# Finishing attention heads without transposing them: inverse sums spread by DMA, scaling on Pool, outputs kept by head columns

## The chip, the core and the metric

The kernel runs on one core of a Trainium2 chip. The core has engines with a queue of instructions each, taken in order: PE (matrix products; PEld in a profile is its loading of weights), DVE (vector work), ACT (scalar functions and copies), POOL (elementwise work) and SP, which here only issues DMAs. Engines wait for each other by semaphores. The metric is the time on the device in microseconds, the median of the runs.

## The reference

Everything is float32. With S = 2048 tokens, D = 576, 32 heads of 18 columns and F = 4608:

```python
xn = _layernorm(x, axis=-1)
qkv = (xn @ wqkv).reshape(B, S, 3, H, Dh).transpose(2, 0, 3, 1, 4)
scores = jnp.einsum("bhqd,bhkd->bhqk", q, k) * (Dh ** -0.5)
p = _softmax(scores, axis=-1)
o = jnp.einsum("bhqk,bhkd->bhqd", p, v)
s = o.transpose(0, 2, 1, 3).reshape(B, S, D) @ wo
b = ((xn @ w_gate) * (xn @ w_up)) @ w_down
return x + s * _silu(b)
```

## The kernel before

Products with long sums split each float32 operand into a high half (rounded to PE's faster format) and a low half (the rest), and sum three products of halves. There are three stages.

The first normalizes x, computes queries, keys and values, and keeps them in DRAM (tensors `sqk`, `sv`). The second, from about 195 us to 2523 us, does the attention of 32 heads and the gated part together. Its order is planned ahead in Python: a loop follows two PE streams and the engines with fixed costs, and emits one operation after the other; `soon`, `moves`, `jobs` and `due` are its lists of work that comes due at some planned time. The third stage is the output product.

For one head, the second stage does: 64 score products whose row maxima DVE takes (`a_item`, L671 and L673, into PSUM banks "a", of which there are two); 64 transposed score products with the maximum folded in, whose exponentials ACT takes (`b_item`, L723 and L725); and in two or so visits (`pv_group`, L734) the products with the values. In a visit PE does up to eight key tiles in a row, each of PE's four groups of 32 columns taking a chunk of 512 queries, and both streams stop for it, so no other product runs beside. The result of a visit is 128x512: partition 32c + d0 + j holds column j of the head for the 512 queries of chunk c, and partition 32c + d0 + 18 holds their sums of exponentials, since `sv` has a column of ones behind each head's 18. Here d0 is 0 for even heads and 13 for odd ones. The first visit of a head is copied to `oc` by ACT (L738), later ones are added by DVE (L740). Between all this stand the products of the gated part (L779 up and gate, L840 down), with their weights loaded on SP (`wgu`, `wd`); in the first six heads or so these weights are also split into halves and stored.

When a head is complete, `finish` (L744 to L766) is put into `jobs`, and the next visit begins with it: DVE transposes `oc` in blocks of 32 (L748), so that tokens stand on partitions, takes the inverse of the sums (L751) and multiplies (L761, put off until Pool is free) into `ot`, which holds two heads. For every second head four DMAs (L756) write `ot` to `so`, a DRAM tensor of [S, D].

The third stage (from L1372 on) goes through 16 tiles of 128 tokens. `fetch_o` (L1381) loads a tile of `so`; ACT repeats the last 64 columns (`join`, L1409); PE transposes five blocks of 128 columns (`columns`, L1417 and L1419); ACT copies the result as the high half (L1421, L1423) and DVE subtracts it to get the low half (L1422, L1424), both into `oT`. Then PE does 28 matmuls with `wo` (L1440) into two of four banks, DVE multiplies with the silu of the gated part, `gin` (L1450), Pool adds x, `xi` (L1455), and Pool's queue stores the result. The silus of the last four token tiles are worked off in small pieces (`chore`, L924 to L934) during the first nine or so tiles.

Memory is handed out by pools that are stacks: the third stage's tiles lie where the second stage's were, and a load into them waits until the old tile there has been read.

Of the kernel before, what the change touches and what calls it, by code (L numbers as in the profile page):

```python
# [41 lines left out]
def kernel(  # L42
# [35 lines left out]
    so = dram.tile([S, D], FT, name="so")  # L78
# [573 lines left out]
    nc.gpsimd.memset(neg.bitcast(FT), 0.0)  # L652
    with ExitStack() as mid:
# [75 lines left out]
        def pv_group(h, ts, k):  # L729
# [6 lines left out]
            if ts[0] == 0:  # L736
                oc[h] = mp.tile([128, 512], FT, name="oc", bufs=1)
                nc.scalar.activation(oc[h], p, AF.Copy)  # L738
            else:
                nc.vector.tensor_tensor(oc[h], oc[h], p, op=OP.add)  # L740

        def finish(h, now):
# [5 lines left out]
            nc.vector.transpose(od.rearrange("p j d -> p (j d)"), o)  # L748
            rc = mp.tile([128, NT, 1], FT, name="rc", bufs=2)
            d0 = 13 * (h % 2)  # L750
            nc.vector.reciprocal(rc, od[:, :, d0 + DH:d0 + DH + 1])  # L751

            def store():
                o = ot.pop(g).rearrange("p j h d -> p j (h d)")
                for c in range(4):
                    nc.sync.dma_start(  # L756
                        so[512 * c:512 * c + 512, g * 2 * DH:(g + 1) * 2 * DH].rearrange("(j q) c -> q j c", q=32),
                        o[32 * c:32 * c + 32])

            def scale(end):  # L760
                nc.vector.tensor_tensor(ot[g][:, :, hh, :], od[:, :, d0:d0 + DH],  # L761
                                        rc.to_broadcast([128, NT, DH]), op=OP.mult)
# [418 lines left out]
        def visit(now):  # L1181

            ends = [j for j in jobs if j[1] is finish]
            for j in ends:
                jobs.remove(j)
                finish(j[2], engine("DVE", max(now, j[0]), 0.93))
# [9 lines left out]
            if many:  # L1196
# [6 lines left out]
                if ts[-1] == NT - 1:  # L1203
                    jobs.append((end + 0.2, finish, h))
# [81 lines left out]
        def order():  # L1286
# [5 lines left out]
            while going(0) or going(1) or na < TOTAL or nb < TOTAL or due or jobs or soon or pool_later:  # L1292
# [11 lines left out]
                if (need and len(due) >= need and due[need - 1][2] <= now  # L1304
                        or any(j[1] is finish for j in jobs) and nb == TOTAL and not due):
                    wait = now if wait is None else wait
                    both = going(0) and going(1)
                    if abs(clk[0] - clk[1]) < 0.04 and next_free("g") - 0.1 <= now + 0.03 or now > wait + 2.0 or not both:
                        visit(now if both else max([now] + [j[0] for j in jobs] + [d[2] for d in due]))
# [65 lines left out]
    with ExitStack() as end:  # L1375
        ep = end.enter_context(tc.tile_pool(name="end", bufs=1, reuse_waits="tile"))
        oin, gin, xi = {}, {}, {}

        def fetch_o(t):
            oin[t] = ep.tile([128, 640], FT, name="oin", bufs=5)  # L1380
            nc.sync.dma_start(oin[t][:, 0:D], so[t * 128:(t + 1) * 128, :])  # L1381
# [17 lines left out]
        for t in order[:2]:  # L1399
            fetch_o(t)  # L1400
        wo_rest()
        for t in order[2:4]:
            fetch_o(t)
        for t in order[:4]:
# [3 lines left out]
        def join(t):  # L1408
            nc.scalar.activation(oin[t][:, D:640], oin[t][:, 512:D], AF.Copy)  # L1409
# [78 lines left out]
```

## Time and profile before

| | |
|---|---|
| median of 3 runs | 2597.2 us (2596.98 to 2598.14) |
| profiled execution, first to last instruction | 2595.7 us |
| DVE: L748, L751, L761 | x32, mean 702, 254 and 508 ns |
| PE: L1417 and L1419 | x64 and x16 |
| SP: L756 | x64 |

A row of the timeline gives start and duration in us, engine and line, the operation, what it writes and reads, shapes, and in brackets the idle time of its engine before it and what ended it. A row of windows gives, for a stretch of time, its length, then for PE, PEld, DVE, ACT and POOL the busy time and in brackets the number of instructions, then the granted clock of PE, the busy share of the 16 DMA engines, and GB/s. SPq is SP's queue: the time that issuing a DMA takes there.

### The profile page before, as it was taken

The page shows a single profiled execution, that of the slowest core. Times are in us where ns is not written, and L with a number is a line of the kernel's source. Part 1 is how long each engine was busy: PE and PEld are TensorE (multiplying, and loading weights), DVE is VectorE, ACT ScalarE, POOL GpSimd, SP SyncE. Part 2 cuts the span into 40 slices and gives each one's busy share as a digit, 9 for nine tenths or more (in the row PEclk, how much of TensorE's full clock was granted, in tenths as well). Part 3 has the DMA queues.
Part 4 walks back from the last instruction along what each step waited for, and adds up shares of the span by engine and source line. Part 5 has one row for each costly group of instructions (what it writes and reads, how often), then busy time and mean ns, then how long its engine had stood idle before and what let it go on. Part 6 is the DMA issues. An engine that isn't in the chain of part 4 may idle for free.

```text
span 2595.7 us, 59551 instructions
## 1 busy us (share of the span) xinstructions
PE 2588.4 (100%) x24520; PEld 2126.7 (82%) x24520; DVE 1786.6 (69%) x2969; ACT 1546.3 (60%) x3107; POOL 671.4 (26%) x694
## 2 busy tenths in 40 slices
PE   9999999999999999999999999999999999999999
PEld 8899877888887778877777888777787878877889
DVE  7209777766777777777777777777777777777236
ACT  4223677766776656665665766656666666666622
POOL 3114444434431222211111222111221222112015
PEclk9999999999999999999999999999999999999999
DMA  7899767677653435444554444343544453433366
GB/s 242 252 300 257 203 182 197 183 191 215 175 191 108 151 134 173 150 142 158 156 174 131 147 139 142 131 139 131 165 166 116 140 146 130 147 130 119 133 208 211
DMA packets 207696, 435.12 MB, mean 168 GB/s; under 512 B 83168, under 2 KB 132992, under 8 KB 177216
## 3 DMA queue, kind: packets, MB, share of 16 engines
q1 hardware_dynamic: 205264, 423.35, 53.5%
q0 software_dynamic: 2160, 7.96, 0.8%
q8 instruction: 193, 3.16, 0.5%
q14 instruction: 79, 0.65, 0.1%
HBM read 314.64 MB, written 111.35 MB: 164 GB/s over the span
## 4 chain that ended last, share of the span: by engine, by line
PE 97%; DVE 1%; DMA 1%; ACT 0%; issue 0%; ACTq 0%; SPq 0%
PE pg L779 36%; PE pg L734 17%; PE pg L840 16%; PE pa L671 11%; PE pb L723 9%; PE pg L1440 2%; PE pg L520 2%; PE pb L463 2%; PE pa L463 1%; DMA sqk<-hl 1%; DVE st L358 0%; PE pb L1417 0%; DVE xn L369 0%; PE pa L723 0%; PE pb L336 0%; DVE mx L673 0%
## 5 line engine op out<-in xcount | busy, mean ns | idle before, releaser
L673 DVE TENSOR_REDUCE mx<-pa 128x1 f32<-128x512 f32 x2016 | 1350.8, 687 | 356.3 <-PE pb L723 172.5
L725 ACT ACTIVATE pt<-pb 128x512 f32<-128x512 f32 x2001 | 1147.2, 603 | 487.8 <-PE pb L723 385.3
L779 PE MATMUL pg<-xc,wgu 64*128 64x512 f32 x7776 | 1391.9, 392 | 0.1
L779 PEld LDWEIGHTS pg<-xc,wgu 64*128 64x128 f32 x7776 | 1049.9, 186 | 54.1 <-issue 0.8
L840 PE MATMUL pg<-wd,hs 64*128 64x288 f32 x6816 | 822.9, 293 | 0.0
L671 PE MATMUL pa<-whole,turning 54*128 54x512 f32 x1999 | 783.2, 398 | 0.1
L840 PEld LDWEIGHTS pg<-wd,hs 64*128 64x128 f32 x6816 | 773.8, 185 | 9.8 <-issue 0.8
L723 PE MATMUL pb<-whole,turning 56*128 56x512 f32 x1977 | 774.4, 398 | 0.0
L734 PE MATMUL pg<-pt,vt 128*32 128x512 f32 x4096 | 453.3, 594 | 0.1
L820 POOL TENSOR_TENSOR hs<-us,hs 128x512 fp32r<-128x512 f32 x144 | 186.2, 1293 | 980.4 <-ACT hs L804 732.1
L671 PEld LDWEIGHTS pa<-whole,turning 54*128 54x128 f32 x1999 | 363.5, 184 | 78.0 <-issue 53.0
L723 PEld LDWEIGHTS pb<-whole,turning 56*128 56x128 f32 x1977 | 359.6, 184 | 7.0 <-ACT pt L725 0.2
L734 PEld LDWEIGHTS pg<-pt,vt 128*32 128x32 f32 x4096 | 126.2, 110 | 285.5 <-issue 279.2
L867 POOL TENSOR_TENSOR acc<-acc,st 128x288 f32<-128x288 f32 x281 | 227.1, 811 | 488.1 <-ACT st L897 283.8
L740 DVE TENSOR_TENSOR oc<-oc,pg 128x512 f32<-128x512 f32 x35 | 24.1, 687 | 220.8 <-PE pg L734 220.8
L257 POOL TENSOR_TENSOR wgu<-wraw,wgu 128x384 fp32r<-128x384 f32 x108 | 108.2, 1015 | 215.2 <-ACT wgu L256 120.6
L738 ACT ACTIVATE oc<-pg 128x512 f32<-128x512 f32 x32 | 19.2, 598 | 230.2 <-PE pg L734 230.2
L903 DVE TENSOR_TENSOR acc<-acc,pg 128x288 f32<-128x288 f32 x264 | 118.0, 448 | 36.0 <-PE pg L840 32.3
L796 DVE TENSOR_TENSOR us<-pg,us 128x512 f32<-128x512 f32 x144 | 98.3, 683 | 47.7 <-PE pg L779 34.1
L897 ACT ACTIVATE st<-pg 128x288 f32<-128x288 f32 x281 | 115.9, 413 | 24.1 <-PE pg L840 18.0
L789 ACT ACTIVATE us<-pg 128x512 f32<-128x512 f32 x141 | 84.4, 598 | 73.9 <-PE pg L779 60.5
L804 ACT ACTIVATE hs<-us 128x512 fp32r<-128x512 f32 x142 | 89.1, 627 | 11.9 <-DVE us L796 11.8
(150 smaller groups left out, 1293.7 us busy)
## 6 DMA issues: line engine op xcount, KB each, us to landing
wgu<-swg SPq DMA_DIRECT2D x102, 1152.0 KB
wd<-swd SPq DMA_DIRECT2D x50, 1152.0 KB
swg<-wgu SPq DMA_DIRECT2D x36, 1152.0 KB
whole<-sqk SPq DMA_DIRECT2D x192, 144.0 KB
turning<-sqk SPq DMA_DIRECT2D x384, 72.0 KB
swd<-wd SPq DMA_DIRECT2D x18, 1152.0 KB
sqk<-hl SPq DMA_DIRECT2D x32, 512.0 KB
xc<-sx SPq DMA_DIRECT2D x24, 512.0 KB
```

Of the source, the lines that this page charges most:

```text
L257: nc.gpsimd.tensor_tensor(w[:, 9 + b:12 + b, :], raw[:, b:b + 3, :], w[:, b:b + 3, :].bitcast(FT), op=OP.subtract)
L671: nc.tensor.matmul(p, q[rows, t * 128:(t + 1) * 128], k[rows, c * 512:(c + 1) * 512], start=True, stop=True)
L673: nc.vector.tensor_reduce(mx[h][:, t, c:c + 1], p, axis=AX.X, op=OP.max)
L723: nc.tensor.matmul(p, k[rows, t * 128:(t + 1) * 128], q[rows, c * 512:(c + 1) * 512], start=True, stop=True)
L725: nc.scalar.activation(pt[t, c // 2][:, c % 2, :], p, AF.Exp, scale=scale)
L734: nc.tensor.matmul(p[32 * c:32 * c + 32, :], vt[h // 2][:, t, 6 * (h % 2):6 * (h % 2) + 32], pt[t, c // 2][:, c % 2, :], start=t == ts[0], ...
L779: nc.tensor.matmul(ps, gw[n][half[r], a, :], xg[i][half[r], e, :], start=k == 0, stop=k == len(TERMS) - 1)
L820: nc.gpsimd.tensor_tensor(hj[:, 1, :], h32, hj[:, 0, :].bitcast(FT), op=OP.subtract)
L840: op = nc.tensor.matmul(ps[:, 0:HALF], hs[u][half[r], j, a, s * 128:(s + 1) * 128], dw[u][half[r], j, e, i * HALF:(i + 1) * HALF], start=( ...
L867: nc.gpsimd.tensor_tensor(a, a, st, op=OP.add)
L897: nc.scalar.activation(st, ps[:, 0:HALF], AF.Copy)
L903: nc.vector.tensor_tensor(a, a, ps[:, 0:HALF], op=OP.add)
```

## The change

At a head's end nothing is transposed any more. `finish` is called as soon as the last visit's addition is planned, and works with `oc` as it stands, columns on partitions:

1. `collect`: four DMAs on SP bring the four rows of sums (512 numbers each) to a tile of 128x16, `lt`.
2. `invert`: DVE takes the inverses of that tile into `rt`.
3. `keep`: a DMA stores them as a row of a DRAM tensor `srl`.
4. `spread`: four DMAs load that row, each chunk repeated on 18 partitions, into `share`, a 128x512 tile that was filled with ones once.
5. `scaled`: Pool multiplies `oc` by `share`.
6. `store`: four DMAs write the head's 18 rows to `sot`, a DRAM tensor of [D, S].

Each step comes due when the plan takes the step before it as done. `oc` has two buffers instead of one, and the planning loop goes on until every head is stored. In the third stage a tile of `sot` is loaded by three DMAs with the columns already on partitions; `join`, `columns` and the transpositions go, and ACT and DVE split from SBUF (`parts`), two tiles ahead, with three `oT` instead of two. The third stage's pool begins with an unused tile of 6080 numbers, so its other tiles lie elsewhere, and the first loads come in another order.

```diff
-    so = dram.tile([S, D], FT, name="so")
+    sot = dram.tile([D, S], FT, name="sot")
+    srl = dram.tile([H, S], FT, name="srl")
...
+    share = accp.tile([128, 512], FT, name="share")
+    nc.gpsimd.memset(share, 1.0)
...
         def finish(h, now):
-            g, hh = divmod(h, 2)
-            o = oc.pop(h)
-            if hh == 0:
-                ot[g] = accp.tile([128, NT, 2, DH], FT, name="ot", bufs=1)
-            od = mp.tile([128, NT, 32], FT, name="od", bufs=1)
-            nc.vector.transpose(od.rearrange("p j d -> p (j d)"), o)
-            rc = mp.tile([128, NT, 1], FT, name="rc", bufs=2)
-            d0 = 13 * (h % 2)
-            nc.vector.reciprocal(rc, od[:, :, d0 + DH:d0 + DH + 1])
+
+            o, d0 = oc.pop(h), 13 * (h % 2)
+            finishing.add(h)
+            sums_of = mp.tile([128, 16], FT, name="lt", bufs=1)
+            inverse_of = mp.tile([128, 16], FT, name="rt", bufs=1)
+
+            def collect():
+                for c in range(4):
+                    row = 32 * c + d0 + DH
+                    nc.sync.dma_start(sums_of[32 * c:32 * c + 32, :],
+                                      o[row:row + 1, :].rearrange("o (a j) -> o a j", j=16))
+                soon.append((moved(now + 0.1, 0.01) + 1.0, "DVE", 0.15, invert))
+
+            def invert(end):
+                nc.vector.reciprocal(inverse_of, sums_of)
+                move(end + 0.1, lambda: keep(end + 0.1))
+
+            def keep(at):
+                nc.sync.dma_start(srl[h].rearrange("(p j) -> p j", j=16), inverse_of)
+                at = moved(at, 0.01) + 1.0
+                move(at, lambda: spread(at))
+
+            def spread(at):
+                for c in range(4):
+                    row = 32 * c + d0
+                    nc.sync.dma_start(share[row:row + DH, :],
+                                      srl[h:h + 1, 512 * c:512 * c + 512].to_broadcast([DH, 512]))
+                soon.append((moved(at, 0.15) + 1.0, "POOL", 1.30, scaled))
+
+            def scaled(end):
+                nc.gpsimd.tensor_tensor(o, o, share, op=OP.mult)
+                move(end + 0.1, store)
 
             def store():
-                o = ot.pop(g).rearrange("p j h d -> p j (h d)")
                 for c in range(4):
-                    nc.sync.dma_start(
-                        so[512 * c:512 * c + 512, g * 2 * DH:(g + 1) * 2 * DH].rearrange("(j q) c -> q j c", q=32),
-                        o[32 * c:32 * c + 32])
-
-            def scale(end):
-                nc.vector.tensor_tensor(ot[g][:, :, hh, :], od[:, :, d0:d0 + DH],
-                                        rc.to_broadcast([128, NT, DH]), op=OP.mult)
-                if hh == 1:
-                    move(end + 0.1, store)
-
-            soon.append((now, "DVE+", 0.53, scale))
+                    row = 32 * c + d0
+                    nc.sync.dma_start(sot[h * DH:(h + 1) * DH, 512 * c:512 * c + 512], o[row:row + DH, :])
+                finishing.discard(h)
+
+            move(now + 0.1, collect)
...
                 if ts[-1] == NT - 1:
-                    jobs.append((end + 0.2, finish, h))
+                    finish(h, end)
...
+        ep.tile([128, 6080], FT, name="room", bufs=1)
...
         def fetch_o(t):
-            oin[t] = ep.tile([128, 640], FT, name="oin", bufs=5)
-            nc.sync.dma_start(oin[t][:, 0:D], so[t * 128:(t + 1) * 128, :])
+            oin[t] = ep.tile([128, 5, 128], FT, name="oin", bufs=5)
+            tokens = slice(t * 128, (t + 1) * 128)
+            nc.sync.dma_start(oin[t][:, 0:4, :], sot[0:512, tokens].rearrange("(k p) s -> p k s", p=128))
+            for b in (0, 64):
+                nc.sync.dma_start(oin[t][b:b + 64, 4, :], sot[512:576, tokens])
...
-        def columns(t):
+        def parts(t):
             o = oin.pop(t)
-            oc = ep.tile([128, 9, 128], FR, name="oT", bufs=2)
-            oT[t] = oc
-            p = bank("b", 2)
-            for k in range(4):
-                nc.tensor.transpose(p[:, k * 128:(k + 1) * 128], o[:, k * 128:(k + 1) * 128], ident)
...
+            oc = oT[t] = ep.tile([128, 9, 128], FR, name="oT", bufs=3)
+            nc.scalar.activation(oc[:, 0:4, :], o[:, 0:4, :], AF.Copy)
+            nc.scalar.activation(oc[:, 8, :], o[:, 4, :], AF.Copy)
+            nc.vector.tensor_tensor(oc[:, 4:8, :], o[:, 0:4, :], oc[:, 0:4, :].bitcast(FT), op=OP.subtract)
+            nc.vector.tensor_tensor(oc[64:128, 8, :], o[64:128, 4, :], oc[64:128, 8, :].bitcast(FT),
+                                    op=OP.subtract)
```

Lines move by 3 at L671 to L740 (L743 is the old L740, L676 the old L673), by 21 at L779 to L966 and by 7 at L1440 to L1459.

What the plan makes of it on DVE, at the end of one head in the middle (mx: row maxima of the next head; us: the product of up and gate; acc: sums of the down product). Before:

```order
L673 TENSOR_REDUCE mx<-pa 128x1 x6
L740 TENSOR_TENSOR oc<-oc,pg 128x512
L673 TENSOR_REDUCE mx<-pa 128x1 x5
L796 TENSOR_TENSOR us<-pg,us 128x512
L673 TENSOR_REDUCE mx<-pa 128x1 x11
L796 TENSOR_TENSOR us<-pg,us 128x512
L673 TENSOR_REDUCE mx<-pa 128x1 x3
L903 TENSOR_TENSOR acc<-acc,pg 128x288
L673 TENSOR_REDUCE mx<-pa 128x1
L903 TENSOR_TENSOR acc<-acc,pg 128x288
L673 TENSOR_REDUCE mx<-pa 128x1 x12
L748 STREAM_TRANSPOSE od<-oc 128x512
```

And now, for a head in the middle:

```order
L924 TENSOR_TENSOR acc<-acc,pg 128x288
L743 TENSOR_TENSOR oc<-oc,pg 128x512
L676 TENSOR_REDUCE mx<-pa 128x1 x5
L762 RECIPROCAL rt<-lt 128x16
L676 TENSOR_REDUCE mx<-pa 128x1 x12
L817 TENSOR_TENSOR us<-pg,us 128x512
```

Before, more than 30 instructions lie between a head's last addition and its transposition; now five lie between the addition and the reciprocal, which waits for the four collects.

On SP, for the same head now (lt, srl, share and sot are the four steps above; wgu and wd are weights of the gated part, whole and turning queries and keys):

```order
L757 DMA lt<-oc 32x1x16 x4
L287 DMA wd<-swd 128x2304
L766 DMA srl<-rt 128x16
L773 DMA share<-srl 18x512 x4
L323 DMA turning<-sqk 18x1024 x3
L662 DMA vt<-sv 128x16x38
L248 DMA wgu<-swg 128x2304
L323 DMA whole_1180<-sqk 18x2048 x3
L784 DMA sot<-oc 18x512 x4
```

Before, at this place SP had, in one piece and for every second head:

```order
L659 DMA vt<-sv 128x16x38
L322 DMA turning<-sqk 18x1024 x3
L286 DMA wd<-swd 128x2304
L756 DMA so<-ot 32x16x36 x4
L247 DMA wgu<-swg 128x2304
L322 DMA turning<-sqk 18x1024 x3
```

Four DMAs in one place have become thirteen in four places, each of which waits for another engine or for the DMA before it.

On DVE in the third stage, now, from the first two tiles on (gl: a silu of the last four tiles):

```order
L1433 TENSOR_TENSOR oT<-oin,oT 128x512
L1434 TENSOR_TENSOR oT<-oin,oT 64x128
L1457 TENSOR_TENSOR y<-pg,gin 128x288 x2
L948 TENSOR_SCALAR gl<-gl 128x576
L952 RECIPROCAL gl<-gl 128x144
L1433 TENSOR_TENSOR oT<-oin,oT 128x512
L1434 TENSOR_TENSOR oT<-oin,oT 64x128
L1457 TENSOR_TENSOR y<-pg,gin 128x288 x2
L952 RECIPROCAL gl<-gl 128x144 x3
```

The order of the kinds is the old one; the low halves read `oin` in SBUF where they read a PSUM bank (pb, pa).

More of the change, by code (lines that the diff above doesn't have):

```diff
@@ L1181, in visit @@
         def visit(now):
[L1183 to L1186, printed above, removed]
             if not due:
@@ L1303, in order @@
                 need = wanted() if next_free("g") < 1e9 else 0
-                if (need and len(due) >= need and due[need - 1][2] <= now
-                        or any(j[1] is finish for j in jobs) and nb == TOTAL and not due):
+                if need and len(due) >= need and due[need - 1][2] <= now:
                     wait = now if wait is None else wait
@@ L1308, in order @@
                     if abs(clk[0] - clk[1]) < 0.04 and next_free("g") - 0.1 <= now + 0.03 or now > wait + 2.0 or not both:
-                        visit(now if both else max([now] + [j[0] for j in jobs] + [d[2] for d in due]))
+                        visit(now if both else max([now] + [d[2] for d in due]))
                         wait = None
```

30 lines of the change are left out of this document (9 added, 21 removed).

## The prediction

> **What bounds the kernel now.** I read the page first, then the chain of waits, then the timeline around one head's end, then the timeline and the windows of the last 75 us.
>
> ```profile
> span 2595.7 us, 59551 instructions
> PE 2588.4 (100%) x24520; PEld 2126.7 (82%) x24520; DVE 1786.6 (69%) x2969; ACT 1546.3 (60%) x3107; POOL 671.4 (26%) x694
> PE 97%; DVE 1%; DMA 1%; ACT 0%; issue 0%; ACTq 0%; SPq 0%
> ```
>
> PE is busy throughout and is 97% of the chain. DVE is busy for 69% of the span, so time taken off DVE is worth something only where PE stands waiting for DVE. Two places matter: the end of each head, 32 times, and the output product after the last down product (L840). The end of a head in the kernel before, from the timeline (start, duration, engine, line):
>
> ```profile
> 1673.74 0.69 DVE L740 TENSOR_TENSOR oc<-oc,pg 128x512 f32<-128x512 f32 x1 [6.60 <-PE pg L734]
> 1674.35 9.06 DVE L673 TENSOR_REDUCE mx<-pa 128x1 f32<-128x512 f32 x13
> 1675.26 0.39 PE L671 MATMUL pa<-whole,turning 54*128 54x512 f32 x1
> 1675.96 0.39 PE L671 MATMUL pa<-whole,turning 54*128 54x512 f32 x1
> 1676.66 0.40 PE L671 MATMUL pa<-whole,turning 54*128 54x512 f32 x1
> ...
> 1700.62 7.07 PE L734 MATMUL pg<-pt,vt 128*32 128x512 f32 x64
> 1701.30 0.70 DVE L748 STREAM_TRANSPOSE od<-oc 128x512 f32<-128x512 f32 x1
> 1702.04 0.25 DVE L751 RECIPROCAL rc<-od 128x16 f32<-128x16 f32 x1
> 1702.33 0.46 DVE L761 TENSOR_TENSOR ot<-od,rc 128x288 f32<-128x288 f32 x1
> 1702.81 2.04 SPq L756 DMA_DIRECT2D so<-ot  x4
> ```
>
> Two things are to be seen. The finish of the head (transposition, inverse, scaling) does not follow its last addition (L740); it runs 27 us later, inside the 7.07 us of the next head's first PV visit, when DVE has nothing else to do. And right after L740, DVE does 13 max-reductions without a gap, 9.06/13 = 0.697 us each. Their ends (1675.05, 1675.74, 1676.44) are each followed by the next score product (L671), which overwrites one of the two banks, 0.21 to 0.22 us later. There DVE is the pace, and PE has some 0.2 us of slack.
>
> **Part 1, what is removed at a head's end: worth 0.** By the rows the three take 0.70 + 0.25 + 0.46 = 1.41 us a head, 45 us in all. They are covered by the PV visit above: DVE begins at 1701.30 and is done at 1702.79, PE is in L734 until 1707.69. Without that cover they would cost up to 45 us; with it, taking them off gives nothing.
>
> **Part 2, what is added there.** Each head now has 13 DMAs on SP (4 collect the sums, 1 stores the inverses, 4 spread them, 4 store the head) where every second head had 4; a reciprocal on DVE (128x16, as L751, 0.25 us); and a product on Pool (128x512; L820, of the same shape, takes 1.29 us). The order shows where the reciprocal stands: not in a PV visit but behind the first few reductions after L743 (the old L740), where DVE is the pace. In 14 heads five instructions of a reduction's length stand between the two (5 x 0.697, less the 0.08 by which the first reduction begins before L740 ends: 3.4 us), in 10 heads six of them or one long inverse more (some 3.8 to 4.1), in 6 nine or more, and in the last two one, where no score products are left to be late. DVE takes its instructions in order, so if the four collects land later than that, every reduction behind the reciprocal is late, and PE with it. The nearest transfer is L709, also a few partitions from SBUF to SBUF:
>
> ```profile
> L820 POOL TENSOR_TENSOR hs<-us,hs x144: 1272/1292/1551, 206.5 to 2511.8; 128x512 fp32r<-128x512 f32 x144
> L709 SPq DMA_DIRECT2D whole<-mr x64: 514/582/1885, 241.1 to 2413.7; - x64
> 948.32 1.15 SPq L709 DMA_DIRECT2D whole<-mr  x2
> 948.90:949.50 0.60, 0.60 (x10) 0.60 (x9) 0.60 (x2) 0.60 (x2) 0.00 (x0) 1.00 0.01 2
> 949.50:950.40 0.90, 0.90 (x15) 0.88 (x13) 0.77 (x3) 0.86 (x3) 0.03 (x1) 1.00 0.07 17
> 950.40:952.00 1.60, 1.60 (x19) 1.60 (x18) 1.46 (x3) 1.21 (x3) 1.51 (x2) 1.00 0.00 0
> ```
>
> One issue holds SP for 0.58 us (min/median/max in ns in its row), so the fourth collect starts 3 x 0.58 = 1.74 us after the first. In the windows (the last two figures are the DMA share and GB/s) the packets of two issues are gone by 950.40, 1.5 us after the second began. The collects are therefore through between 1.74 + 1.5 = 3.2 us, with no time for the signal, and, with the one row that shows issue to reading of a load (first issue 2516.85, read at 2519.82, quoted below), 1.74 + 3.0 = 4.7 us. That load moved 288 KB, a collect 2 KB, so I take the lower half: 3.7 us. A short head then waits 3.7 - 3.4 = 0.3 us, and every head has the reciprocal's 0.25. Less the 0.2 us of slack, a short head costs 0.35, a middle one 0.05, a long one nothing. Of the 14 short heads 11 come after the sixth: 11 x 0.35 + 7 x 0.05 = 4 us, between 0 and 11 x (4.7 - 3.4 + 0.05) = 15.
>
> The first six heads are different, since weights are still split and stored then. Four us of DMA after the last addition of heads 0 and 2, and of a later one:
>
> ```profile
> 331.60:335.60 4.00, 4.00 (x38) 3.28 (x36) 3.92 (x7) 3.96 (x9) 1.01 (x1) 1.00 0.88 268
> 472.50:476.50 4.00, 4.00 (x41) 3.68 (x39) 3.80 (x7) 3.35 (x7) 0.00 (x0) 1.00 1.03 406
> 1674.00:1678.00 4.00, 4.00 (x38) 3.36 (x36) 3.89 (x7) 3.26 (x6) 0.00 (x0) 1.00 0.01 4
> 2508.14 9.03 SPq L1381 DMA_DIRECT2D oin<-so  x2
> 2515.96 0.26 ACT L1409 ACTIVATE oin<-oin 128x64 f32<-128x64 f32 x1 [4.29 <-DMA oin<-so]
> 2516.85 0.32 SPq L1381 DMA_DIRECT2D oin<-so  x1
> 2519.82 0.26 ACT L1409 ACTIVATE oin<-oin 128x64 f32<-128x64 f32 x1 [3.59 <-DMA oin<-so]
> ```
>
> The engines are at 0.88 to 1.03 there, against 0.01 later, and the order puts only 3.4 to 4.1 us of work ahead of the reciprocal. A load behind a full queue took 2515.96 - 2508.14 = 7.8 us from issue to reading, against 3.0 for the one issued at 2516.85. So the collects are 0 to 4.8 us later than the 3.7 above. I take 1.2, a quarter of the way, because the queue is part empty by then: 6 x (1.2 + 0.05) = 7.5 us, between 0 and 6 x 4.85 = 29.
>
> The Pool product and the other nine DMAs I cost at 1 us, between 0 and 32 x 0.26 x half of 1.29 = 5: Pool is 26% busy, and the order puts the product among the low halves (L820) for which down products wait, so a late spread delays one of them now and then. On SP the next weight loads stand behind the waiting spread; they are needed a whole up and gate product later. Sum of part 2: 4 + 7.5 + 1 = **+12.5 us**, between 0 and 49.
>
> **Part 3, the output product.** Per token tile PE now does five transpositions and 28 matmuls:
>
> ```profile
> 2522.98 0.66 PE L1417 MATMUL pb<-identr,oin 128*128 128x128 f32 x4
> 2524.33 0.79 PE L1440 MATMUL pg<-wos,oT 128*128 128x288 f32 x4
> ...
> 2541.10 0.60 PE L1417 MATMUL pb<-identr,oin 128*128 128x128 f32 x4
> 2541.54 3.74 PEld L1440 LDWEIGHTS pg<-wos,oT 128*128 128x128 f32 x28
> 2545.35 0.60 PE L1417 MATMUL pb<-identr,oin 128*128 128x128 f32 x4
> ```
>
> The period is 2545.35 - 2541.10 = 4.25 us, of which the 28 weight loads take 3.74. Without the transpositions a tile takes 3.75, 0.5 less, and 15 times that is 7.5 us; at the start PE spends 2522.98 to 2524.33 on the columns of two tiles and waits for ACT, of which I count 0.7 us as saved, since the low half still comes after DVE's last additions. That is 8.2 us if nothing else becomes the pace. Two things could. DVE, first:
>
> ```profile
> 2550.00:2560.00 10.00, 10.00 (x80) 10.00 (x79) 9.84 (x15) 3.30 (x10) 6.08 (x9) 1.00 0.86 274
> L761 DVE TENSOR_TENSOR ot<-od,rc x32: 394/458/1476, 349.8 to 2493.7; 128x288 f32<-128x288 f32 x32
> L927 DVE TENSOR_SCALAR gl<-gl x4: 451/1406/2302, 2528.9 to 2559.3; 128x576 f32<-128x576 f32 x4
> ```
>
> While the last four silus are worked off, DVE is busy 9.84 of 10 us (third engine in the row), 9.84 x 4.25/10 = 4.2 us a tile, more than the new 3.75. Also, L761 (both inputs in SBUF) and L927 take up to three and five times their shortest; the new low halves (L1433, L1434) have both inputs in SBUF too, while Pool is busy 6.08 of 10. Over the eight or nine tiles concerned DVE falls behind by 0.45 us or more each, some 4 us; four banks let PE run two tiles ahead, which takes up half. I cost it at 2 us, between 0 and the whole 8. The Trainium skill's "GPSIMD Engine Reference", section "1. Specifications", says that Pool and DVE share their way to SBUF and that DVE instructions with two SBUF inputs contend for it; the 1476 ns of L761 agree. DMA, second:
>
> ```profile
> 410.50:412.50 2.00, 2.00 (x26) 2.00 (x25) 2.00 (x5) 2.00 (x5) 1.01 (x1) 1.00 0.93 203
> 639.00:641.00 2.00, 2.00 (x26) 1.99 (x25) 1.91 (x4) 2.00 (x6) 1.72 (x2) 1.00 1.19 244
> 2528.00:2530.00 2.00, 2.00 (x18) 2.00 (x17) 1.43 (x3) 0.77 (x2) 0.94 (x2) 1.00 1.03 386
> ```
>
> The first two windows hold loads of weights in rows of 128 numbers (512 bytes), the third loads of whole token rows (2304 bytes). The new loads of outputs come in 512-byte pieces, 640 of them, 328 KB: at 203 to 244 GB/s 1.3 to 1.6 us, where 295 KB at 386 took 0.76. With gin, xi and the store of the result (3 x 0.76) that is 3.6 to 3.9 us a tile against PE's 3.75. Just enough, and loads run four tiles ahead, so 0, at most 12 x 0.15 = 2. The Trainium skill's "DMA: Bandwidth & Descriptors", section "Specifications", gives 512 bytes as enough for the full rate, by which the load would run at 386 GB/s as well and DMA would need, as an estimate, 328/386 + 2.3 = 3.1 us a tile and could not decide; the rows differ, and they decide. Sum of part 3: **-6 us**, between 0 and -8.2.
>
> **The sum.** 2595.7 + 12.5 - 6 = 2602.2 us of span; the median of the runs lies 1.5 us above this span, so 2603.7. I put it at 2603.
>
> **The rivals.**
> - *The collects land in time.* If they are through by 3.4 us and the first six heads find room, part 2 shrinks to about 1 us and the tail shows: 2597.2 + 1 - 8 = 2590. For it: the packets of L709 are gone 1.5 us after issue. Against it: four issues in a row, and the shares of 0.88 to 1.03. It decides once a collect's issue takes 0.5 us or less.
> - *The first six heads pay the full queue.* At 3 us each instead of 1.25 they cost 18: 2597.2 + 4 + 18 + 1 - 6 = 2614. For it: 7.8 us behind a full queue. Against it: the later windows of these heads are partly empty.
> - *The tail gains nothing*, DVE or the 512-byte loads being its pace: 2597.2 + 12.5 - 1 = 2609. For it: 9.84 of 10 us; against: only the first nine tiles have silus.
> - That DVE's 45 us come off the span (2550) I give nothing: they lie under L734.
>
> **How the numbers follow.** Forecast 0.42 (2603, its own range 2598 to 2608), collects in time 0.28 (2590), full queue 0.18 (2614), no gain in the tail 0.12 (2609). The range 2590 to 2616 leaves out half of the first rival's lower side and the upper bounds of part 2. About 0.2%, 5 us, is what a measurement of this kernel can tell from no change. Slower than 2602.4: over half of the forecast (0.24) and nearly all of the last two (0.27), 0.51; faster than 2592: most of the first rival, 0.25; between: 0.24.
>
> **What would show it.** Right: the reciprocal L762 waits on the DMA of the collects for 0.2 to 0.5 us in most heads and longer in the first six, and the first L676 after it starts late by that; the period of L1447 near 3.75 us, no L1417. Wrong: L762 shows no wait (first rival); L762 waits over 2 us up to 700 us (second); L1447 keeps near 4.2 us (third). The sum is wrong altogether if the PE order makes PE wait at places that neither part touches.

## The result, and the profile after

| | before | after |
|---|---|---|
| median | 2597.3 us (2596.98 to 2598.14, 4 runs) | 2614.1 us (2613.44 to 2621.23, 4 runs) |
| after to before | | 1.0070, 95% interval 1.0056 to 1.0084 |
| profiled execution | 2595.7 us | 2619.5 us |

The change made the kernel 17 us slower. The profiled execution, of 2619.5 us, is 7 to 8 us longer than the other three (2611.7 to 2612.4 us); half of what sets it apart is shown below. The page of after, with span, busy time by engine and shares of the chain of waits:

```profile
span 2619.5 us, 60107 instructions
PE 2596.8 (99%) x24440; PEld 2129.6 (81%) x24440; DVE 1752.8 (67%) x2899; ACT 1551.8 (59%) x3097; POOL 717.3 (27%) x732
PE 91%; DMA 4%; DVE 3%; SPq 1%; issue 1%; POOL 0%; ACT 0%; DVEq 0%; ACTq 0%; POOLq 0%
```

DVE has 34 us less work than before and the span is longer. The chain of waits, 97% PE before, now has 4% DMA and 3% DVE. The windows of the second and the third stage, before and then after:

```profile
194.70:2522.90 2328.20, 2327.76 (x22942) 1890.58 (x22942) 1669.65 (x2731) 1466.29 (x2912) 592.29 (x595) 1.00 0.52 158
2522.90:2595.70 72.80, 69.04 (x530) 68.15 (x528) 50.18 (x87) 16.55 (x50) 37.90 (x49) 1.00 0.68 226
```

```profile
195.10:2551.50 2356.40, 2344.47 (x22942) 1902.88 (x22942) 1630.57 (x2661) 1472.83 (x2917) 635.48 (x632) 1.00 0.51 159
2551.50:2619.50 68.00, 60.95 (x450) 59.60 (x448) 55.75 (x87) 15.39 (x36) 40.42 (x49) 0.98 0.74 239
```

The tail gained 72.8 - 68.0 = 4.8 us. The main stage, with the same 22942 matmuls, lost 28.2. Of these, 11.5 are time in which PE shows nothing at all (11.9 idle against 0.4). The rest passes while PE looks busy.

**The idle time** stands behind the reciprocal. First what it waits for (us, times), then PE's largest wait in the second stage (us, times, longest), which was 0.1 us at the same line before:

```profile
L762 DVE RECIPROCAL rt<-lt x32: 241/253/255, 336.6 to 2495.9; 128x16 f32<-128x16 f32 x32
  DMA lt<-oc: 13.1, 16
```

```profile
PE pa L674 <- DVE mx L676: 8.8, 10, 2.2
```

The worst head end, DVE's rows of the timeline and then the chain of waits of the same stretch:

```profile
1759.79 0.69 DVE L743 TENSOR_TENSOR oc<-oc,pg 128x512 f32<-128x512 f32 x1 [6.39 <-PE pg L737]
1760.39 3.38 DVE L676 TENSOR_REDUCE mx<-pa 128x1 f32<-128x512 f32 x5
1766.24 0.25 DVE L762 RECIPROCAL rt<-lt 128x16 f32<-128x16 f32 x1 [2.46 <-DMA lt<-oc]
1766.41 1.22 DVE L676 TENSOR_REDUCE mx<-pa 128x1 f32<-128x512 f32 x2
```

```profile
1762.36 3.70 DMA lt<-oc
...
1766.24 0.25 DVE rt L762
1766.49 0.56 DVE mx L676
1767.05 0.04 issue
1767.09 0.58 PE pa L674
```

After the last addition there are 3.4 us of reductions, as the prediction has it, and then DVE stands 2.46 us for the fourth collect. The first reduction behind the reciprocal releases PE's next score product at 1767.09. Microsecond by microsecond around that stop (after the five engines: clock, DMA share, GB/s):

```profile
1764.00:1765.00 1.00, 0.88 (x9) 0.49 (x6) 0.00 (x0) 1.00 (x3) 0.68 (x1) 1.00 0.01 0
...
1766.00:1767.00 1.00, 0.00 (x0) 0.00 (x0) 0.76 (x3) 0.00 (x0) 0.00 (x0) 1.00 0.00 0
1767.00:1768.00 1.00, 0.91 (x6) 0.91 (x8) 0.74 (x3) 0.02 (x1) 0.00 (x0) 0.58 0.09 8
1768.00:1769.00 1.00, 1.00 (x9) 1.00 (x8) 0.58 (x1) 0.54 (x2) 0.53 (x1) 0.50 0.00 0
1769.00:1770.00 1.00, 1.00 (x9) 1.00 (x7) 0.41 (x1) 0.69 (x2) 0.27 (x1) 0.50 0.00 0
1770.00:1771.00 1.00, 1.00 (x8) 0.82 (x8) 0.83 (x3) 0.36 (x1) 0.00 (x0) 0.72 0.00 0
```

Two things are to be read. The DMA engines are empty (0.01, 0.00) while the collect is still out, so here it does not wait behind other traffic. And after PE's stop its granted clock is half for some 3.4 us, which loses 0.42 + 0.50 + 0.50 + 0.28 = 1.7 us more. This happened twice in the profiled execution (also after 1193, where the DMA engines were not empty: 0.78 to 1.02), 3.4 of its 7 extra us. The Trainium skill's "TensorE: Matmul & The Clock Gate", section "Part 1: The HAM clock gate (the "warmup" mystery)", describes such a halving after an idle window of 3413 ns that runs freely; the length of the halving agrees, and stops of PE of 2.14 and 2.21 us were enough here.

### The profile page after: what moved, and what is told of

Its sections match the earlier page's. It is cut to its first block, busy times and chain, and to the rows that moved or that the text cites. A ratio compares the mean times of both kernels' runs of the same rounds, so it can differ in the third digit from the quotient of the medians.

```text
span 2619.5 us, 60107 instructions
## 1 busy us (share of the span) xinstructions
PE 2596.8 (99%) x24440; PEld 2129.6 (81%) x24440; DVE 1752.8 (67%) x2899; ACT 1551.8 (59%) x3097; POOL 717.3 (27%) x732
## 4 chain that ended last, share of the span: by engine, by line
PE 91%; DMA 4%; DVE 3%; SPq 1%; issue 1%; POOL 0%; ACT 0%; DVEq 0%; ACTq 0%; POOLq 0%
PE pg L800 34%; PE pg L737 17%; PE pg L861 15%; PE pa L674 10%; PE pb L726 9%; PE pg L521 2%; PE pb L464 2%; PE pa L464 1%; DMA lt<-oc 1%; DMA sqk<-hl 1%; SPq L757 1%; DMA oin<-sot 1%; DMA xi<-in_A_x_dram 1%; DVE mx L676 0%; DVE st L359 0%
## 5 line engine op out<-in xcount | busy, mean ns | idle before, releaser
L676 DVE TENSOR_REDUCE mx<-pa 128x1 f32<-128x512 f32 x2016 | 1349.4, 686 | 389.1 <-PE pb L726 187.3
L800 PE MATMUL pg<-xc,wgu 64*128 64x512 f32 x7776 | 1418.4, 392 | 0.6 <-DMA wgu<-swg 0.5
L800 PEld LDWEIGHTS pg<-xc,wgu 64*128 64x128 f32 x7776 | 1061.2, 186 | 49.7 <-issue 0.8
L861 PE MATMUL pg<-wd,hs 64*128 64x288 f32 x6816 | 844.5, 294 | 1.2 <-DVEq L865 1.1
L861 PEld LDWEIGHTS pg<-wd,hs 64*128 64x128 f32 x6816 | 785.9, 186 | 11.4 <-DVEq L865 1.5
L743 DVE TENSOR_TENSOR oc<-oc,pg 128x512 f32<-128x512 f32 x35 | 24.1, 688 | 229.0 <-PE pg L737 229.0
```

The source lines that it names most:

```text
L676: nc.vector.tensor_reduce(mx[h][:, t, c:c + 1], p, axis=AX.X, op=OP.max)
L800: nc.tensor.matmul(ps, gw[n][half[r], a, :], xg[i][half[r], e, :], start=k == 0, stop=k == len(TERMS) - 1)
L861: op = nc.tensor.matmul(ps[:, 0:HALF], hs[u][half[r], j, a, s * 128:(s + 1) * 128], dw[u][half[r], j, e, i * HALF:(i + 1) * HALF], start=( ...
```

## The experiments

Theory A: the loss is DVE's wait for the collects and PE behind it. Theory B: it is Pool's product and the other DMAs. Theory C: it is PE's new order, since the plan, told other times, wrote PE's whole program in another order. The first four kernels keep the changed kernel's PE order word for word, so they price A, B and C apart. The expectations call the changed kernel's 2614 by its rounded number; each run's ratio is to runs of the kernel before on the same chip (medians 2596.9 to 2597.5).

### No wait

```diff
+    unit = accp.tile([128, 16], FT, name="unit")
+    nc.gpsimd.memset(unit, 1.0)
...
-                nc.vector.reciprocal(inverse_of, sums_of)
+                nc.vector.reciprocal(inverse_of, unit)
```

> Leaves out: the inverses are taken of a constant tile of ones instead of the collected sums, so the heads are not normalised. All DMAs, the reciprocals, the Pool products and PE's order stay as in the changed kernel; only DVE's wait for the collects is gone. Theory A (the 17 us are DVE waiting in its queue for the collects, 13.1 us in the trace, and PE behind it): 2592 to 2600. Theory B (the Pool product and the spread and store DMAs delay low halves and weight loads): at least 2608. Theory C (PE's new order itself is worse): at least 2606.

Measured: 2601.3 us (2599.97 to 2603.37), ratio 1.0016 (1.0007 to 1.0025). The wait costs 2614.1 - 2601.3 = 12.8 us, the larger part of the loss. But 2601.3 is a little over theory A's 2592 to 2600: something else is left.

### The reciprocal four reductions later

```diff
-                nc.vector.reciprocal(inverse_of, sums_of)
                 move(end + 0.1, lambda: keep(end + 0.1))
+                move(end + 2.0, late)
+
+            def late():
+                nc.vector.reciprocal(inverse_of, sums_of)
+                nc.sync.dma_start(srl[h].rearrange("(p j) -> p j", j=16), inverse_of)
...
-                nc.sync.dma_start(srl[h].rearrange("(p j) -> p j", j=16), inverse_of)
```

> Computes everything. The reciprocal and the DMA behind it are written 2 us of the plan later, behind four more reductions; PE's, ACT's and Pool's order stay as they are. The fourth collect landed 3.5 to 3.8 us after its head's last addition in most heads and 5.4 to 6.7 in the latest; the reciprocal would now be reached after 6.2 us or so. Theory A: the waits shrink to nearly nothing, 2593 to 2601. Theory B and C: within 3 us of 2614.

Measured: 2604.0 us (2602.93 to 2606.2), ratio 1.0027 (1.0016 to 1.0037). No wait for a collect is left at its reciprocal, and 10 us are back by moving one instruction and the DMA behind it. It missed theory A's upper bound of 2601 by 3 us, in part for the same reason as above; why it is 2.7 us slower than the kernel without the wait was not seen.

### No store, spread and product

```diff
-                nc.sync.dma_start(srl[h].rearrange("(p j) -> p j", j=16), inverse_of)
...
-                for c in range(4):
-                    row = 32 * c + d0
-                    nc.sync.dma_start(share[row:row + DH, :], ...
...
-                nc.gpsimd.tensor_tensor(o, o, share, op=OP.mult)
```

> Leaves out: the store of the inverses, their spread and the Pool product are not issued (heads are stored unscaled); the collects, the reciprocal with its wait and PE's order stay. Theory A: 2610 to 2614. Theory B: 2592 to 2600. Theory C: at least 2606.

Measured: 2611.8 us (2608.49 to 2613.85), ratio 1.0057 (1.0043 to 1.0070). Theory B falls: taking away everything it blames gives back 2.3 us.

### The order alone

The edits of the last kernel, and the collects and the reciprocal left out as well.

> Leaves out: collects, reciprocals, stores and spreads of the inverses and Pool products are not issued (heads are stored unscaled); PE's order, the stores of heads and the new output product stay. It gives the price of the order and of the tail alone. Theory A: 2590 to 2593 (2597.3 less 4.8 to 6 for the tail, and nothing for the order). Theory B: the same. Theory C: at least 2602.

Measured: 2600.0 us (2599.07 to 2601.12), ratio 1.0011 (1.0003 to 1.0020), 7 us over the 2590 to 2593 of theories A and B, and 2 under the 2602 of theory C. With the tail's 4.8 us taken off the 2596.9 of before one expects 2592.1. So PE's order (with the stores of the heads, the only thing added that is left) costs 7.9 us, and Pool's product, the collects and the other DMAs, without a wait, 2601.3 - 2600.0 = 1.3. The window of its main stage, to be read beside the two above, says the same without the medians:

```profile
194.70:2530.90 2336.20, 2335.27 (x22944) 1907.19 (x22942) 1628.10 (x2629) 1470.51 (x2919) 595.10 (x600) 1.00 0.51 158
```

It is 8.0 us longer than before, and PE is idle for 0.9 us of it, against 0.4.

### The old order with the new finish

The plan of before is put back: the finish begins in the next head's visit, with the old reserved times, so PE's main stage is word for word the old one. The steps that are issued are the new ones.

```diff
-                    finish(h, end)
+                    jobs.append((end + 0.2, finish, h))
+                    move(end + 0.3, lambda: collect(h))
...
+            nc.vector.reciprocal(inverse_of, lots.pop(h))
...
+            move(now + 0.3, keep)
+            move(now + 3.3, spread)
+            move(now + 7.0, scaled)
+            move(now + 8.5, store)
+            soon.append((now, "DVE+", 0.53, lambda end: None))
```

> Computes everything. The plan is that of the kernel before (the finish of a head stands in the next head's first visit, with the same reserved times), so PE's order of the main stage is word for word the old one; what is issued is the new finish: collects right after the head's last addition, the reciprocal in the next visit, then store, spread, Pool product and stores. The tail is the new one. If the 7.5 us that the order alone cost (2600.0 with everything left out, against 2597.3 less 4.8 for the tail) come from PE's changed order: 2592 to 2595 (2597.0 - 4.8 + about 1.3 for Pool and DMAs). If they come from the stores of the heads or from the tail's new loads meeting the main stage, which are kept: 2599 to 2603.

Measured: 2619.1 us (2617.93 to 2621.65), ratio 1.0084 (1.0071 to 1.0098), a miss on both sides. Its own waits show why, first PE's, then what Pool's product waited for (us, times, for PE the longest too):

```profile
PE pg L859 <- POOLq L863: 16.5, 4, 8.0
```

```profile
  DMA share<-srl: 210.5, 23
```

Pool's product was written too early: it waited 210 us for its spread (16.3 in the changed kernel, whose plan gives it a time), Pool takes its instructions in order, and four times the low halves behind it kept PE, once for 8 us, with the clock halved after. Head by head (time less a fixed price per matmul), this kernel lost 20.9 us in heads 2 to 5 and 4.0 after the last head; the heads between lost 0.7 in sum. That the old order is free of loss elsewhere was visible, but not yet a time.

### One collect

```diff
-                for c in range(4):
-                    row = 32 * c + d0 + DH
-                    nc.sync.dma_start(sums_of[32 * c:32 * c + 32, :],
-                                      o[row:row + 1, :].rearrange("o (a j) -> o a j", j=16))
+                nc.sync.dma_start(sums_of, o[d0 + DH:d0 + DH + 97:32, :].rearrange("c (a j) -> c a j", j=16))
```

> Computes everything. The four collects of a head become one DMA over the four partitions; all engines but SP keep the changed kernel's order. If the wait is the chain of four issues (0.62 us each, the fourth begins 1.87 us after the first, each lands 1.7 us after its issue): landing after 1.7 to 2.2 us, before the 3.4 us of work ahead of the reciprocal, so no wait, 2601 to 2604 as with the later reciprocal. If a collect lands late because of what it moves (128 small pieces in one DMA instead of 32): within 3 us of 2614.

Measured: 2601.1 us (2600.44 to 2605.07), ratio 1.0016 (1.0007 to 1.0025). The one DMA completes 1.9 us after its issue in most heads, where the fourth of a chain completed 3.5 to 3.7 us after the first was issued. The same source view as above, of this kernel, has no line of idle time under the reciprocal. So the four issues in a row were the wait, with the late one that now and then was among them.

### The plan told of later sums

```diff
-                soon.append((moved(now + 0.1, 0.01) + 1.0, "DVE", 0.15, invert))
+                soon.append((moved(now + 0.1, 0.01) + 4.0, "DVE", 0.15, invert))
```

> Computes everything. As the kernel with the reciprocal behind four more reductions, but the plan itself is told that the sums come 3 us later, so PE's order changes again as a whole. The waits are gone as there (2604.0 with the changed kernel's order). If the order's 7.5 us are a matter of where the plan happens to fall, this order can be anything from 2593 to 2606; if every plan that doesn't finish a head inside the next visit costs them, it stays at 2602 to 2606.

Measured: 2599.9 us (2597.85 to 2602.53), ratio 1.0009 (1.0000 to 1.0018). Without the wait, and 4 us better than a similar lateness in the changed kernel's order: another order, another price.

### The old order, Pool's product later

```diff
-            move(now + 3.3, spread)
-            move(now + 7.0, scaled)
-            move(now + 8.5, store)
+            at = (5.0, 22.0, 23.5) if h < H - 1 else (8.5, 13.0, 14.5)
+            move(now + at[0], spread)
+            move(now + at[1], scaled)
+            move(now + at[2], store)
```

For the other heads the store of the inverses goes out at once, for the last head the reciprocal and this store come 5 us later.

> Computes everything. The plan of the kernel before again, PE's main stage word for word the old one, but the Pool product now 22 us after the finish in place of 7 (the last head: reciprocal 5 us, product 13 us after). Before, heads 6 to 30 cost nothing against the kernel before (0.0 us each, within 0.1) and the loss of 25.6 us lay in heads 2 to 5 and at the end, where Pool stood at the product waiting for the spread, with PE waiting up to 8.1 us for the low halves behind it. If that early product is all that was wrong there: 2592 to 2596. If the early heads can't hold these DMAs at all: 2600 to 2615.

Measured: 2594.9 us (2593.95 to 2598.59), ratio 0.9991 (0.9982 to 1.0000). Everything is computed and issued, in the old order, and the main stage costs 2594.9 - (2597.5 - 4.8) = 2.2 us more than before. With less issued, in the new order, it cost 7.9. So at least 7.9 - 2.2 = 5.7 us of the loss are the order itself, and theory C holds beside A. The profiled executions agree: the last down product ends at 2525.2 us here and at 2530.9 in the kernel with the order alone.

**What is worse in the new order.** A score, gate or down product takes only 64 or fewer rows of PE, and the two streams of the plan use one half of the rows each; two such products run at once if one of each half is at hand. PE's rows of the timeline of after:

```profile
894.63 0.50 PE L674 MATMUL pa<-whole,turning 54*128 54x512 f32 x1
894.63 0.50 PE L726 MATMUL pb<-whole,turning 56*128 56x512 f32 x1
...
896.56 0.39 PE L726 MATMUL pb<-whole,turning 56*128 56x512 f32 x1
896.79 0.56 PE L861 MATMUL pg<-wd,hs 64*128 64x288 f32 x3
897.15 0.49 PE L674 MATMUL pa<-whole,turning 54*128 54x512 f32 x1
```

At 894.63 two begin in the same instant. From 896.56 to 897.15 one begins after the other, 0.23 us for 512 columns and 0.13 or less each for 288: the program has eight products of one half in a row there, the longest run before the stage's end, and half of PE stands empty while the profile says busy. I counted pairs of neighbours of the same half in the written order, 1612 before and 1782 after, and laid the order out by hand, each product on its half (0.213 us for 512 columns, 0.12 for 288): 1810 us before and 1818 after. The 8 us lie in the first twelve heads. The count alone does not tell it: the plan told of later sums has 1906 such pairs and loses 4.6 us by the layout, and the first of the two plans below has 1822 and loses nothing.

The layout is arithmetic on the program, but the trace of the kernel with the order alone can be held against it. Its time less fixed prices (these two, and 7.07 us for a full visit), over that of before, is 4.9 us after six heads, 7.8 after twelve and 8.6 after fifteen, where the layout has 5.2, 8.4 and 9.0; at later heads the two differ by up to 2.5 us, and at the end of the stage they are 7.9 and 8.2. Two more plans were chosen by the layout (theory D: the order's price is lost pairing).

### Two plans chosen by their pairing

```diff
-                soon.append((moved(now + 0.1, 0.01) + 1.0, "DVE", 0.15, invert))
+                soon.append((moved(now + 0.1, 0.01) + 6.0, "DVE", 0.15, invert))
```

on top of the one collect, and, for the other, + 9.0 there and

```diff
-                soon.append((moved(at, 0.15) + 1.0, "POOL", 1.30, scaled))
+                soon.append((moved(at, 0.15) + 4.0, "POOL", 1.30, scaled))
```

> Computes everything. One collect DMA a head, and the plan is told that the sums come 5 us later than in the changed kernel; nothing else. Theory D: the order's price is how well PE's two halves (rows 0 to 63 and 64 to 127, which work at the same time on two 64-row products) stay paired. Laid out by hand, each product on its half with 0.213 us for 512 columns and 0.12 us for 288, PE's written order of the main stage takes 1810 us in the kernel before, 1818 in the changed one and 1810 here. Then no wait and no lost pairing is left: 2592 to 2596 (2597.3 - 4.8 for the tail + 1.3 for Pool and DMAs + 0). If the pairing is not the cause and this is a kernel like the one with one collect: 2599 to 2603.

> Computes everything. One collect DMA a head, the plan told that the sums come 8 us later and that the spread takes 3 us longer before Pool's product. Laid out by hand as above, PE's written order takes 1811 us. Theory D: 2592 to 2597, and, with Pool's product later, no stop of PE behind a low half. If the pairing is not the cause: 2599 to 2603.

Measured: 2598.9 us (2595.74 to 2602.28), ratio 1.0005 (0.9996 to 1.0014), and 2596.4 us (2594.14 to 2597.69), ratio 0.9996 (0.9987 to 1.0005). The second is where theory D puts it, and both are under the 2601.1 of the kernel with one collect in the order that the layout rates worst. The first missed D's 2596 by 3 us and lies at the edge of the range without D, 2599 to 2603. Its runs spread over 6.5 us: the five with a mean clock of 0.999 take 2598.9 us or more, the six with 1.000 take 2595.7 to 2600.1. A halved clock seems to go with the longer ones, but the profiled execution (2593.9) is among the shortest, so what they wait for was not seen. Pairing has the right size and sign; that it is the whole of the order's price is not settled.

### The tail

In the changed kernel 11 of 15 periods of L1447 take 3.71 to 3.79 us, the others 4.37 to 4.70. DVE's rows around the three long ones that follow each other closely:

```profile
2574.82 0.96 DVE L1433 TENSOR_TENSOR oT<-oin,oT 128x512 fp32r<-128x512 f32 x1
2575.80 1.41 DVE L1434 TENSOR_TENSOR oT<-oin,oT 64x128 fp32r<-64x128 f32 x1
2577.24 0.82 DVE L1457 TENSOR_TENSOR y<-pg,gin 128x288 f32<-128x288 f32 x2
2577.98 0.92 DVE L948 TENSOR_SCALAR gl<-gl 128x576 f32<-128x576 f32 x1
2578.94 1.97 DVE L952 RECIPROCAL gl<-gl 128x144 f32<-128x144 f32 x2
2580.82 0.63 DVE L1433 TENSOR_TENSOR oT<-oin,oT 128x512 fp32r<-128x512 f32 x1
```

One round of DVE takes 6 us here without a gap, against PE's 3.71 a tile, and the small low half takes 1.41 us where its shortest is 0.29. Both kernels below are the last old-order kernel with one collect and a third result tile; one also has this low half on Pool for eight tiles.

```diff
-            nc.vector.tensor_tensor(oc[64:128, 8, :], o[64:128, 4, :], oc[64:128, 8, :].bitcast(FT),
-                                    op=OP.subtract)
+            low = nc.gpsimd if 1 < order.index(t) < 10 else nc.vector
+            low.tensor_tensor(oc[64:128, 8, :], o[64:128, 4, :], oc[64:128, 8, :].bitcast(FT),
+                              op=OP.subtract)
...
-            y = ep.tile([128, D], FT, name="y", bufs=2)
+            y = ep.tile([128, D], FT, name="y", bufs=3)
```

> Computes everything. The kernel before's plan with the late Pool product (2594.9), one collect DMA a head, and in the output product three result tiles in place of two and the small low half (64x128, 0.65 us on average on DVE) on Pool for eight of the tiles. In the changed kernel's tail 11 of 15 tiles take 3.71 to 3.79 us and four take 4.37 to 4.70. If DVE being behind, or waiting for a result tile to be stored, is what makes those four long: they come down to about 3.8, the tail loses 2 to 3 us, 2591.5 to 2593.5. If Pool then slows DVE as much as it takes off it (both read SBUF): 2594 to 2597.

> Computes everything. The same with the small low half on DVE throughout, so only the third result tile and the one collect are new. If the waits for the store of a result tile (6.5 us of DVE's time in the changed kernel's profile) are what counts: 2592 to 2594, as with Pool. If DVE's work is: 2594 to 2595.5.

Measured: 2593.1 us (2591.86 to 2596.2), ratio 0.9985 (0.9976 to 0.9994) with the low half on Pool; 2596.1 us (2594.09 to 2597.78), ratio 0.9994 (0.9985 to 1.0003) without, over both of its ranges. All 15 periods of the first are 3.71 to 3.84 us; the second keeps periods of 4.70 and 4.37, and its first is 5.36. That first one is not DVE's doing. PE stopped for 1.34 us at the start of the stage, and its clock was halved after it, as the timeline and the windows of the second kernel show:

```profile
2528.13 6.04 PE L1453 MATMUL pg<-wos,oT 128*128 128x288 f32 x32 [1.34 <-ACT oT L1436]
```

```profile
2528.00:2529.00 1.00, 0.87 (x4) 0.87 (x5) 0.85 (x2) 0.89 (x4) 0.00 (x0) 0.62 0.22 62
2529.00:2530.00 1.00, 1.00 (x6) 1.00 (x6) 0.94 (x3) 0.92 (x4) 0.00 (x0) 0.50 0.61 182
```

Five of its eleven runs have a mean clock of 0.999 and take 2596.9 to 2597.8 us, the six with 1.000 take 2594.1 to 2596.1. Among the runs with 1.000 the medians of the two kernels are 2593.0 and 2594.9, so about 2 of the 3 us between them are the moved work, and the rest goes with the clock. Pool's group for the moved work, in the tail of the first (busy us, mean ns; then its idle time):

```profile
L1440 POOL TENSOR_TENSOR oT<-oin,oT 64x128 fp32r<-64x128 f32 x8 | 3.8, 474 | 12.7 <-DVE oT L1438 12.2
```

Eight subtractions, 3.8 us on Pool, take the long periods out of the tail. The kernel with them is the fastest of all: 4.5 us under before, 21 under the change.

## Why the prediction was near, and which step failed

The forecast was 2603, with slower the likeliest side; the median, 2614.1, lies at the upper end of its range of 2590 to 2616. The range of the forecast's own path, 2598 to 2608, it leaves by 6 us; that the wide range holds it is luck in part, since 7.9 us of the loss were in no step. By its steps:

| step | predicted | the runs showed |
|---|---|---|
| part 1, work taken off DVE | 0 | no gain seen: DVE has 34 us less, and in the old order the main stage is still 2.2 us longer |
| part 2, wait for the collects | +11.5 | +12.8 |
| part 2, Pool's product and other DMAs | +1 | +1.3 |
| PE's order | no term | +7.9 |
| part 3, output product | -6 | -4.8 |
| sum | +6.5 | +17.2, measured +16.8 |

The last line agrees by construction, since the pieces are differences between neighbouring kernels. The 7.9 alone was seen a second time, in the window of the main stage.

**The step that failed** is one that is not in the sum. The prediction listed under what would make it wrong that "the PE order makes PE wait at places that neither part touches", and gave that no price, no chance and no place. It is the largest difference. Nor does PE wait, so the trace would not have shown it under that name: its idle time in the main stage is 0.4 us before and 0.9 in the kernel with the order alone.

**The wait** had the right sum from the wrong heads. The landing time was right: the fourth collect is seen 3.7 us or so after the last addition, and where no collect was late, short heads behind the first wait 0.6 us or less. The first six heads were to pay 7.5 us for a full queue. They pay 1.26, then 0.45 at most:

```profile
336.61 0.25 DVE L762 RECIPROCAL rt<-lt 128x16 f32<-128x16 f32 x1 [1.26 <-DMA lt<-oc]
407.14 0.25 DVE L762 RECIPROCAL rt<-lt 128x16 f32<-128x16 f32 x1
```

The windows of four us after the last additions of the first two heads, and one line of the waits of SP's queue (us, times, longest), say why:

```profile
331.60:335.60 4.00, 4.00 (x38) 3.36 (x36) 3.67 (x6) 3.78 (x8) 0.57 (x1) 1.00 0.04 6
403.20:407.20 4.00, 4.00 (x38) 3.38 (x36) 3.78 (x8) 4.00 (x9) 1.91 (x2) 1.00 0.12 21
```

```profile
SPq L757 <- DVE oc L743: 184.3, 20, 12.8
```

The DMA share was 0.88 at the first of these places before, and is 0.04 now. SP reaches the collect early and stands there until the addition is done, up to 12.8 us; nothing behind it is issued, and the queue runs empty. The collect makes its own room. I had read the share from a kernel in which SP had no reason to stop. The later heads were to pay 4 us and pay most of the 13. In four of them DVE stood 1.66 to 2.46 us: there a late collect of the four completed up to 2 us after its usual time, in one of them with the DMA engines empty, as shown. No row of before held that. In the kernel with one collect these four heads do not wait.

**The output product.** The period fell from 4.25 to 3.71, as forecast, and DVE fell behind, which I priced at 2 us; the four long periods lose 3.0 (4 x 3.71 = 14.84, against 17.87). Of this 0.7 is the first period, at the start of the stage, which was long before as well (4.47). The last of the 15 periods took 3.79 before already, so only 14 could become shorter. At the end, one loss was not foreseen:

```profile
2614.88 0.46 DVE L1457 TENSOR_TENSOR y<-pg,gl 128x288 f32<-128x288 f32 x1 [3.36 <-DMA out_dram<-y]
```

The last tile's product waits for the store of a result tile; from the last tile's first matmul to the end there are 8.8 us, against 7.6 before and 7.6 with a third result tile. With two result tiles this loss comes and goes: five of the eleven such kernels end in 7.6 or 7.7 us, the others in 8.4 to 8.8. DMA in 512-byte pieces, put at 0, was not the pace: with the small low half on Pool, PE keeps 3.71 us a tile.

**The rivals.** The second gave 2614, the very number, by a mechanism that is refuted; the agreement is chance. The first, the collects in time, is what one DMA makes of them; it then leads to 2601 and not to 2590, for the order's sake. The third, a tail without gain, did not come.

## What to carry to other kernels

Where a plan writes the order of all engines, a change to one engine's work rewrites the others' order too, and that has a price of its own: hold the order fixed in one experiment, and look for lost overlap inside an engine that the profile calls busy. A chain of small DMAs is as late as its number of issues; one DMA with a stride over partitions took 1.9 us where four took 3.6. An instruction that waits for a DMA belongs behind other work of its queue, and a DMA that waits for an engine empties the queue behind it, so queue shares from before don't carry over to after.

## What was not expected of the hardware

- Whether a stop of PE halves its clock depends on where the stop falls. In the traces of all fourteen kernels every change of the granted clock lies on a grid of 3413 ns, counted from the first clock record. The stops of 2.14 and 2.21 us in after, and of 2.28 us at 2517 us in the first old-order kernel, left PE idle for 1.9 to 2.2 us of one interval of that grid, and were followed by a halving. Stops of 2.30 and 2.38 us up to 597 and 672 us in that old-order kernel, and of 2.42 us in the kernel told of later sums, fell into two intervals, at most 1.6 us in one, and were not. One stop does not fit: the 1.34 us in the tail of the last kernel lay in one interval and halved the clock. The freely running window that the Trainium skill states in the section named above agrees with the grid; no run here varied the phase on purpose.
- One of four small DMAs could complete some 2 us after its usual time, once with the DMA engines idle. Its cause is open.
- The subtraction of 64x128 took 290 ns on DVE at the median and 1715 at most, with Pool busy beside; on Pool it took 474 on average.
